# Two lanes of TensorE without zero padding, in a kernel of gated attention followed by a token mixer

## The chip, the cores and the metric

The kernel runs on one core of a Trainium2 chip. That core has TensorE (PE in the profile, with its weight loads listed apart as PEld), VectorE (DVE), ScalarE (ACT), GpSimd (POOL) and SyncE (SP, which here issues DMAs), and 16 DMA engines that move data between main memory and the core's SBUF. TensorE writes its results to PSUM, which has eight banks of 128 rows x 512 fp32 columns here. The metric is the device time of one execution in microseconds (us).

## The reference: what is computed

There are 8 batches of 3200 tokens with 256 features. The first half is an attention without softmax, gated by `u`; the second mixes tokens through two projections:

```
scores = (1/S) * z @ z.T            # z: 3200 x 64 per batch
x      = u * (relu(scores)**2 @ v)  # u, v: 3200 x 256
wq, wk = x @ w_q, x @ w_k           # 256 -> 64
mixed  = ((1/8) * wq @ wk.T) @ x
out    = relu(mixed) @ w_out        # 256 -> 256
```

The output is fp32. The kernel doesn't build `wq @ wk.T`: it sums `wk.T @ x` (64 x 256, called heads) over the tokens of a batch and multiplies `wq` with it.

## The kernel before

**Tiles.** The tokens of a batch are 25 tiles of 128. The columns of the score matrix are taken in groups of 512 (six per batch, and a last one of 128). For a group and a tile of rows, TensorE makes a 128 x 512 block of scores (`scores`, L273, matmul at L284). Two blocks share a buffer `sc` of two PSUM banks. VectorE or ScalarE moves the buffer out with relu and a scale (`first_stage`, L298 or L296, into `g`), and GpSimd or ScalarE squares it to fp16 (`second_stage`, L309 or L307, into `at`). As the score matrix is symmetric, some blocks are got by a transposing DMA from an earlier one (`tt`).

**The second product.** For each group, `second_product` (L432) sums over all 25 tiles of rows: the squared scores are the weights, `v_sb` the moving operand, 256 columns per matmul. A group of 512 fills two accumulator banks, `acc0` and `acc1`. All the recorded matmuls of this kind, and those of the extras below, stand under L346, the `emit` of an item; their tiles tell them apart. When a group closes, `gate` (L456) multiplies the accumulators with `u`: VectorE takes `acc0` (L475), ScalarE copies `acc1` (L474) and GpSimd multiplies it. The next group uses the same two banks, so its first matmul waits for both.

**Two lanes.** Most matmuls use 64 of TensorE's 128 rows: the lower half of a tile's rows is one lane (LOW), the upper half the other (HIGH), and a matmul of one lane runs beside one of the other if they write different banks. So `lanes` (L373) emits a list of items twice. In the first pass lane LOW takes the items of one bank and HIGH those of the other; in the second they change over, so that each bank gets both halves of the rows. `swap_after` (L411) puts between the passes a wait for the last matmul of either lane. The two matmuls of a score buffer are one per lane too, LOW first.

**Extras.** Besides scores and the second product a step may carry one extra, written to a buffer of the same pool as the scores (three buffers, `ps_tile`): `project` (L735) is the last product with `w_out`; `keys_and_heads` (L744) holds the two projections of a group of `x` in one bank (two items of 512 columns, 1024 in all) and in the other the heads of an earlier group (items of 256, mostly four of them) with, at times, the projections of the batch's last 128 tokens or a small remainder of the batch before (`side`). This other bank has 1024 columns or 1280, 1536 or, once, 2048. Where it is not 1024, `evened` (L361) puts items of 128 columns with zeros for the moving operand ahead of the last item of the shorter list, at most four.

**Order of the work.** The schedule is written out by the kernel itself: the instructions of each engine stand in the order in which the program emits them. A loop over 169 steps decides for each what is due. A step emits, in this order: some pairs of scores (`heading` of them, L958 to 961), the squares that are due, then the matmuls of the second product and the extra by `run` (L398), which walks a list of emitters and drops `asides`, the remaining score pairs among them, at given shares of the list's width (`shares_of`, L853). A step that begins a group and has an extra of both banks emits both passes of the extra first, then those of the group; one in the middle of a group puts the first pass of the extra inside the first pass of the group. A step of a batch's last group (128 columns, "split") gives each lane its own partial sum and bank, so that only the extra changes banks there. `on_lanes` (L952) tells the steps that work in this way.

The order of the two lanes within one pass is by column: `lanes` keeps a counter for each lane that begins at zero in each pass, and sorts by it:

```
for i in evened(banks, lane ^ across):
    todo.append((at, lane, i, rows))
    at += width(i)
```

Of the kernel before, what the change touches and what calls it, by code (L numbers as in the profile page):

```python
# [16 lines left out]
def kernel(  # L17
# [15 lines left out]
    P = 128  # L33
    NT = S // P
    ND = D // P
    W = 512
# [162 lines left out]
    zeros = consts.tile([P, P], FP16, tag="zeros", name="zeros")  # L199
# [45 lines left out]
    for b in range(B):  # L245
        for gi in range(NG):
# [23 lines left out]
    NTILE = len(tiles)  # L270
    made, turned = {}, {}

    def scores(p0):  # L273
        pair = tiles[p0 : p0 + 2]
        sc = ps_tile("sc")
        ats = [[], []]
        for h, (b, gi, tis) in enumerate(pair):
            w = widths[gi]
            half = h * dqk
            for i in range(W // w):  # L280
                ti = tis[min(i, len(tis) - 1)]
                ats[h].append((i * w, h, w, b, ti, starts[gi], half))
        for at, h, w, b, ti, gs, half in sorted(ats[0] + ats[1]):
            nc.tensor.matmul(  # L284
                out=sc[:, h, at : at + w],
                lhsT=zT[b][half : half + dqk, ds(z_at(b, h) + ti * P, P)],
                rhs=zT[b][half : half + dqk, ds(z_at(b, h) + gs, w)],
                start=True,
                stop=True,
            )  # L290
        return sc
# [48 lines left out]
    class Item:  # L340
        def __init__(self, out, lhsT, rhs, start=False, stop=False):
            self.out, self.lhsT, self.rhs = out, lhsT, rhs
            self.start, self.stop = start, stop

        def emit(self, rows, start, stop):
            return nc.tensor.matmul(  # L346
                out=self.out, lhsT=self.lhsT(rows), rhs=self.rhs(rows), start=start, stop=stop
            )
# [6 lines left out]
    def width(i):  # L355
        n = 1
        for d in i.out.shape[1:]:
            n *= d
        return n

    def evened(banks, mine):  # L361


        items = list(banks[mine])
        more = sum(map(width, banks[1 - mine])) - sum(map(width, items))
        if more > 0 and items:
            z_ = Item(
                out=items[-1].out[:, 0:P], lhsT=items[-1].lhsT, rhs=lambda r: zeros[r, :]
            )
            items[-1:-1] = [z_] * (min(W, more) // P)  # L370
        return items

    def lanes(banks, across, second, ends_):  # L373


        todo = []
        for lane, rows in enumerate((LOW, HIGH)):
            at = 0
            for i in evened(banks, lane ^ across):
                todo.append((at, lane, i, rows))  # L380
                at += width(i)

        def emit(lane, i, rows):
            ends_[lane] = i.emit(rows, i.start and not second, i.stop and second)

        return [
            (width(i) / 2, lambda lane=lane, i=i, rows=rows: emit(lane, i, rows))
            for _, lane, i, rows in sorted(todo, key=lambda x: x[:2])
        ]

    def both_lanes(banks):
        return [
            (width(i) / 2, lambda i=i, rows=rows: i.emit(rows, i.start, i.stop))
            for both in zip(*banks)
            for i, rows in zip(both, (LOW, HIGH))
        ]

    def run(emits, asides_):  # L398


        total, done = sum(n for n, _ in emits), 0
        asides_ = sorted(asides_, key=lambda x: x[0])
        for n, fn in emits:
            while asides_ and asides_[0][0] * total <= done:
                asides_.pop(0)[1]()
            fn()
            done += n
        for _, fn in asides_:
            fn()
# [426 lines left out]
    def key_due(k):  # L836
# [53 lines left out]
    def each(fns):  # L890
        for fn in fns:
            fn()
# [36 lines left out]
    across = False  # L929
# [3 lines left out]
    while groups:  # L933
# [3 lines left out]
        n = 6  # L937
# [7 lines left out]
        if mix_due(k):  # L945
# [3 lines left out]
            n = 4  # L949
# [87 lines left out]
        if on_lanes:  # L1037
            split = is_split(b, gi)
            if extra and not all(extra[0]):
                for fn in whole(extra[0]):  # L1040
                    fn()
                extra[1]()
                extra = None
            parts = [] if split else [banks]
            if extra and not begins and not split:
                n_ = max(2, min(len(banks[0]) - 2, len(banks[0]) // 2))
                parts = [[bank[:n_] for bank in banks], extra[0], [bank[n_:] for bank in banks]]
            elif extra:
                parts.insert(0, extra[0])
            emits = []  # L1050
            apart = extra and begins and not split
            if apart:
                turned_ = {}
                emits += lanes(extra[0], across, False, turned_)
                first_done = sum(n for n, _ in emits)
                emits.append((0, lambda: swap_after(turned_.values())))
                emits += lanes(extra[0], not across, True, {})
                emits.append((0, extra[1]))
                parts = [banks]
            firsts = [{} for part in parts]  # L1060
            for part, ends_ in zip(parts, firsts):
                emits += lanes(part, across, False, ends_)
            if len(parts) == 3:
                parts, firsts = [extra[0], banks], firsts[1:]
            cut = len(rows_) // 4
            if split:
                emits += both_lanes([bank[:cut] for bank in banks])
            halves_ = sum(n for n, _ in emits)
            if parts:
                across = not across  # L1070
            for part, ends_ in zip(parts, firsts):
                emits.append((0, lambda ends_=ends_: swap_after(ends_.values())))
                emits += lanes(part, across, True, {})
                if extra and not apart and part is extra[0]:
                    emits.append((0, extra[1]))
            if split:
                emits += both_lanes([bank[cut:] for bank in banks])
            at_ = shares(begins, closes, split, len(between_))
            if apart:
                all_ = sum(n for n, _ in emits)  # L1080
                at_ = [(n - 1) / all_ for n in (first_done, halves_, halves_)][: len(between_)]
            todo = [(x, lambda p0=p0: stage(p0, scores(p0))) for x, p0 in zip(at_, between_)]
            for x in acts[1:]:
                todo.append((0.5 - 1e-6, lambda x=x: each(second_stage(*x))))
            run(emits, todo)
# [158 lines left out]
```

## Time and profile before

| | |
|---|---|
| runs shown | 784.98, 785.11 and 782.51 us, median 784.98 |
| the profiled execution | 782.56 us, span of its instructions 780.7 us |
| granted TensorE clock | 0.998 of full speed |
| matmuls | 12690, busy 768.5 us |
| matmuls of zeros under L346 | 148 (104 with `wkq`, 44 with `wqk`) |
| DMA | 147.05 MB, q1 86.3% of 16 engines' span |

The span is shorter than the execution by 1.9 us that lie around it. A group of the profile names line, engine, operation, the tile written and those read, the shape (64*128 means 64 rows in use and 128 columns of weights; 64x256 is the moving operand) and the count; then the busy time, the mean time of one in ns, and the engine's idle time ahead of them. Matmuls are pipelined: one of 256 columns is recorded with 269 ns, but the next of the same lane starts 0.109 us after it. The timeline merges equal neighbours: start, length, then the operation and its count; in square brackets, the idle time before it and what ended it.

### The profile page before, as it was taken

Reading aid. Unit: us, or ns where it says so; the run is one execution under the profiler, and the core shown is the slowest. Engines: PE = TensorE matmul, PEld = TensorE weight load, DVE = VectorE, ACT = ScalarE, POOL = GpSimd, SP = SyncE. Lnnn points to the kernel's source line nnn. Section 1 sums busy time; section 2 is a strip of 40 time slices with the busy share of each in tenths; the row PEclk is TensorE's granted clock in tenths of the full one; section 3 lists DMA queues with packets and bytes.
Section 4 is the critical chain, followed back from the end, with each engine's and each line's share of the span. In section 5 each row is a group of like instructions: output and inputs, shape, how many; then the busy total and the mean of one; then the engine's idle time right before and its main releaser. Section 6 shows DMA issues by size and latency. Waiting matters only on the chain. (4 is left out here: it accounts for less than half of the span.)

```text
span 780.7 us, 28613 instructions
## 1 busy us (share of the span) xinstructions
PE 768.5 (98%) x12690; PEld 627.3 (80%) x12690; DVE 473.5 (61%) x457; ACT 556.9 (71%) x655; POOL 554.9 (71%) x363
## 2 busy tenths in 40 slices
PE   8999999999999999999999999999999999999996
PEld 6788877888788887888878887788878888888884
DVE  7654676556756577555766557655575646665444
ACT  7666787767768786685867667758696877685465
POOL 7897797758765678765879668876777546875450
PEclk9999999999999999999999999999999999999999
DMA  8999699896999479994899959999499994987626
GB/s 172 173 221 231 132 211 188 172 185 127 237 180 230 123 166 221 229 256 112 186 203 239 219 143 217 203 221 245 99 218 183 255 205 94 211 193 151 160 68 254
DMA packets 276267, 147.05 MB, mean 188 GB/s; under 512 B 252080, under 2 KB 255664, under 8 KB 276144
## 3 DMA queue, kind: packets, MB, share of 16 engines
q1 hardware_dynamic: 275424, 143.33, 86.3%
q0 software_dynamic: 576, 1.64, 1.2%
q8 instruction: 99, 1.62, 0.9%
q14 instruction: 24, 0.20, 0.1%
q10 hardware_dynamic: 144, 0.26, 0.1%
HBM read 59.38 MB, written 26.21 MB: 110 GB/s over the span
## 5 line engine op out<-in xcount | busy, mean ns | idle before, releaser
L298 DVE TENSOR_SCALAR g<-sc 128x1024 f32<-128x1024 f32 x338 | 410.7, 1223 | 241.7 <-PE sc L284 227.7
L309 POOL TENSOR_TENSOR at<-g 128x1024 f16<-128x1024 f32 x238 | 448.0, 1894 | 122.9 <-DVE g L298 100.1
L346 PE MATMUL acc<-v_sb,at 64*128 64x256 f16 (+1 forms) x7387 | 474.5, 269 | 1.8 <-DVE x_sb L475 0.7
L346 PEld LDWEIGHTS <-at 64*128 64x128 f16 (+1 forms) x7387 | 364.9, 94 | 87.4 <-PE acc L346 25.0
L307 ACT ACTIVATE at<-g 128x1024 f16<-128x1024 f32 x230 | 239.2, 1055 | 29.4 <-DVE g L298 17.6
L346 PE MATMUL acc<-v_sb,tt 64*128 64x256 f16 (+1 forms) x2540 | 174.8, 269 | 0.0
L284 PE MATMUL sc<-zT 64*128 64x512 f16 (+1 forms) x1104 | 168.6, 344 | 1.6 <-ACT g L296 0.8
L296 ACT ACTIVATE g<-sc 128x1024 f32<-128x1024 f32 x130 | 133.0, 1023 | 41.4 <-PE sc L284 39.3
L346 PEld LDWEIGHTS <-tt 64*128 64x128 f16 (+1 forms) x2540 | 127.2, 94 | 15.0
L477 POOL TENSOR_TENSOR x_sb<-gt,u_sb 128x512 f16<-128x512 f32 x48 | 61.2, 1275 | 72.7 <-ACT gt L474 65.3
L611 ACT ACTIVATE rt<-mx 128x1024 f16<-128x1024 f32 x47 | 47.8, 1023 | 34.4 <-PE mx L590 32.3
L284 PEld LDWEIGHTS <-zT 64*128 64x128 f16 x1104 | 55.5, 94 | 11.2 <-issue 3.9
L474 ACT COPY gt<-acc 128x512 f32<-128x512 f32 x48 | 28.1, 585 | 48.6 <-PE acc L346 48.5
L346 PE MATMUL fo<-wo,rt 64*128 64x256 f16 (+1 forms) x688 | 58.2, 270 | 0.1
L346 PE MATMUL qk<-x_sb,kx 64*128 64x256 f16 x368 | 55.2, 269 | 0.0
L512 ACT CAST qk<-qk 128x512 f16<-128x512 f32 x47 | 27.5, 586 | 37.3 <-PE qk L346 37.2
L475 DVE TENSOR_TENSOR x_sb<-acc,u_sb 128x512 f16<-128x512 f32 x48 | 33.1, 690 | 26.7 <-PE acc L346 25.3
L346 PEld LDWEIGHTS <-rt 64*128 64x128 f16 (+1 forms) x688 | 35.9, 94 | 15.2 <-PE fo L346 5.1
L672 ACT ACTIVATE fo<-fo 128x1024 f32<-128x1024 f32 x39 | 39.9, 1024 | 4.3 <-PE fo L346 4.3
L346 PEld LDWEIGHTS <-kx 64*128 64x128 f16 (+1 forms) x386 | 35.5, 94 | 7.6 <-PE qk L346 0.9
L346 PE MATMUL qk<-xT_sb,wkq 64*128 64x512 f16 (+1 forms) x90 | 31.8, 377 | 0.0
L346 PE MATMUL qk<-xT_sb,wqk 64*128 64x512 f16 (+1 forms) x94 | 30.1, 377 | 0.0
(81 smaller groups left out, 268.9 us busy)
## 6 DMA issues: line engine op xcount, KB each, us to landing
u_sb<-in_u_dram SPq DMA_DIRECT2D x48, 512.0 KB, 5.1
out_dram<-fo SPq DMA_DIRECT2D x45, 512.0 KB, 3.4
piece<-in_v_dram SPq DMA_DIRECT2D x42, 512.0 KB, 4.6
piece<-in_z_dram SPq DMA_DIRECT2D x7, 512.0 KB, 5.9
tt<-at SPq DMA_TRANSPOSE x162, 4.8
piece<-in_z_dram SPq DMA_DIRECT2D x7, 288.0 KB, 5.5
out_dram<-fo SPq DMA_DIRECT2D x5, 256.0 KB, 2.7
u_sb<-in_u_dram SPq DMA_DIRECT2D x8, 128.0 KB, 3.3
```

The source lines that it names most:

```text
L284: nc.tensor.matmul(out=sc[:, h, at : at + w], lhsT=zT[b][half : half + dqk, ds(z_at(b, h) + ti * P, P)], rhs=zT[b][half : half + dqk, ds(z ...
L296: nc.scalar.activation(out=g[:], in_=sc[:], func=RELU, scale=GSCALE)
L298: nc.vector.tensor_scalar(out=g[:], in0=sc[:], scalar1=0.0, scalar2=GSCALE, op0=AOP.max, op1=AOP.mult)
L307: nc.scalar.square(out=out, in_=g[:])
L309: nc.gpsimd.tensor_mul(out=out, in0=g[:], in1=g[:])
L346: return nc.tensor.matmul(out=self.out, lhsT=self.lhsT(rows), rhs=self.rhs(rows), start=start, stop=stop)
L474: nc.scalar.copy(out=upper[:], in_=accs[1][:])
L475: nc.vector.tensor_mul(out=x[:, 0:n], in0=accs[0][:, 0:n], in1=ug[:, 0:n])
L477: nc.gpsimd.tensor_mul(out=x[:, n : 2 * n], in0=upper[:], in1=ug[:, n : 2 * n])
L512: nc.scalar.copy(out=qks[b, gi][:, 0:gw], in_=out)
L611: nc.scalar.activation(out=out, in_=ps[:], func=RELU)
L672: nc.scalar.mul(out=flat_out[:, sl], in_=part, mul=FINAL_SCALE)
```

## The change

Three things are changed. `evened` goes, and with it the zeros. The emitters of a step are no longer lists that are joined: a new class, `Streams`, keeps one counter of columns for each lane over the whole step and sorts all matmuls by the column at which their lane can begin them; `first_pass` and `second_pass` add the two passes of a part, and a second pass doesn't begin before the column at which both lanes have ended the first one. A step that begins a group with an extra of unequal banks now adds the first pass of the extra, the first pass of the group, the second pass of the extra and the second pass of the group; with equal banks the order is as it was.

The score pair of an aside begins with the lane that has been given fewer columns so far (`lead`). For a step that begins a group with keys and heads, the share of the first aside is 0.0 instead of 0.5, and one more pair of scores goes ahead of the step if a `side` is waiting.

```diff
-    def scores(p0):
+    def scores(p0, lead=0):
...
-        for at, h, w, b, ti, gs, half in sorted(ats[0] + ats[1]):
+        for at, h, w, b, ti, gs, half in sorted(ats[0] + ats[1], key=lambda x: (x[0], x[1] ^ lead)):
...
-    def evened(banks, mine):
-        items = list(banks[mine])
-        more = sum(map(width, banks[1 - mine])) - sum(map(width, items))
-        if more > 0 and items:
-            z_ = Item(
-                out=items[-1].out[:, 0:P], lhsT=items[-1].lhsT, rhs=lambda r: zeros[r, :]
-            )
-            items[-1:-1] = [z_] * (min(W, more) // P)
-        return items
-    def lanes(banks, across, second, ends_):
...
-    def both_lanes(banks):
...
+    class Streams:
+        def __init__(self):
+            self.at, self.todo = [0, 0], []
+        def add(self, lane, n, fn):
+            self.todo.append((self.at[lane], len(self.todo), n, lane, fn))
+            self.at[lane] += n
+        def aside(self, at, fn):
+            self.todo.append((at, len(self.todo), 0, 0, fn))
+        def ordered(self):
+            return [x[2:] for x in sorted(self.todo, key=lambda x: x[:2])]
+    def first_pass(streams, banks, across):
+        ends_ = {}
+        def emit(lane, i, rows):
+            ends_[lane] = i.emit(rows, i.start, False)
         for lane, rows in enumerate((LOW, HIGH)):
...
+            for i in banks[lane ^ across]:
+                streams.add(lane, width(i), lambda lane=lane, i=i, rows=rows: emit(lane, i, rows))
+        return banks, across, max(streams.at), ends_
+    def second_pass(streams, first):
+        banks, across, done, ends_ = first
+        streams.at = [max(at, done) for at in streams.at]
+        streams.aside(min(streams.at), lambda: swap_after(ends_.values()))
+        for lane, rows in enumerate((LOW, HIGH)):
+            for i in banks[1 - (lane ^ across)]:
+                streams.add(lane, width(i), lambda i=i, rows=rows: i.emit(rows, False, i.stop))
+    def uneven(extra):
+        a, b = (sum(map(width, bank)) for bank in extra[0])
+        return a != b
...
+    def run(streams, asides_):
+        todo = streams.ordered()
+        total, done = sum(x[0] for x in todo), [0, 0]
         asides_ = sorted(asides_, key=lambda x: x[0])
...
+        for n, lane, fn in todo:
+            while asides_ and asides_[0][0] * total <= sum(done):
+                asides_.pop(0)[1](int(done[1] < done[0]))
             fn()
...
+            done[lane] += n
...
-        "bk": (0.5, 0.5, 0.5),
+        "bk": (0.0, 0.5, 0.5),
...
+            if begins and keying and side: heading += 1
...
+            if split:
+                cut = len(rows_) // 4
+                if extra:
+                    first = first_pass(streams, extra[0], across)
+                    across = not across
+                each_lane(streams, [bank[:cut] for bank in banks])
+                if extra:
+                    extra_second(first)
+                each_lane(streams, [bank[cut:] for bank in banks])
+            elif extra and begins and uneven(extra):
+                first_extra = first_pass(streams, extra[0], across)
+                first = first_pass(streams, banks, across)
+                extra_second(first_extra)
+                second_pass(streams, first)
+                across = not across
...
             elif extra:
...
                 n_ = max(2, min(len(banks[0]) - 2, len(banks[0]) // 2))
...
+                first = first_pass(streams, [bank[:n_] for bank in banks], across)
+                first_extra = first_pass(streams, extra[0], across)
+                first = (banks, across) + first_pass(streams, [bank[n_:] for bank in banks], across)[2:]
+                extra_second(first_extra)
+                second_pass(streams, first)
                 across = not across
```

More of the change, by code (lines that the diff above doesn't have):

```diff
@@ L402, in run, with each_lane @@
+    def uneven(extra):
+        a, b = (sum(map(width, bank)) for bank in extra[0])
+        return a != b
+    def each_lane(streams, banks):
+        for lane, rows in enumerate((LOW, HIGH)):
+            for i in banks[lane]:
+                streams.add(lane, width(i), lambda i=i, rows=rows: i.emit(rows, i.start, i.stop))
+    def run(streams, asides_):
+        todo = streams.ordered()
+        total, done = sum(x[0] for x in todo), [0, 0]
         asides_ = sorted(asides_, key=lambda x: x[0])
-        for n, fn in emits:
-            while asides_ and asides_[0][0] * total <= done:
-                asides_.pop(0)[1]()
+        for n, lane, fn in todo:
+            while asides_ and asides_[0][0] * total <= sum(done):
+                asides_.pop(0)[1](int(done[1] < done[0]))
@@ L406, in run @@
             fn()
-            done += n
+            done[lane] += n
         for _, fn in asides_:
-            fn()
+            fn(0)
     def swap_after(ends_):
@@ L1043 @@
                 extra = None
-            parts = [] if split else [banks]
-            if extra and not begins and not split:
-                n_ = max(2, min(len(banks[0]) - 2, len(banks[0]) // 2))
[L1047 to L1069, printed above, removed]
-                across = not across
[L1071 to L1082, printed above, removed]
+            streams = Streams()
+            at_ = shares(begins, closes, split, len(between_))
@@ new lines, in extra_second @@
+            def extra_second(first):
+                second_pass(streams, first)
+                streams.aside(max(streams.at) - 1, extra[1])
+            if split:
[13 more added lines that the diff above has]
+                across = not across
+            elif extra and begins:
+                first = first_pass(streams, extra[0], across)
+                marks = [max(streams.at)]
+                extra_second(first)
+                first = first_pass(streams, banks, across)
+                marks.append(max(streams.at))
+                second_pass(streams, first)
+                across = not across
+                marks = [2 * x for x in marks]
+                total = sum(x[2] for x in streams.todo)
+                at_ = [(x - 1) / total for x in marks + marks[1:]][: len(between_)]
+            elif extra:
+                n_ = max(2, min(len(banks[0]) - 2, len(banks[0]) // 2))
+                first = first_pass(streams, [bank[:n_] for bank in banks], across)
+                first_extra = first_pass(streams, extra[0], across)
+                first = (banks, across) + first_pass(streams, [bank[n_:] for bank in banks], across)[2:]
+                extra_second(first_extra)
+                second_pass(streams, first)
+                across = not across
+            else:
+                second_pass(streams, first_pass(streams, banks, across))
+                across = not across
@@ L1083 @@
+            todo = [(x, lambda lead, p0=p0: stage(p0, scores(p0, lead))) for x, p0 in zip(at_, between_)]
             for x in acts[1:]:
-                todo.append((0.5 - 1e-6, lambda x=x: each(second_stage(*x))))
-            run(emits, todo)
+                todo.append((0.5 - 1e-6, lambda lead, x=x: each(second_stage(*x))))
+            run(streams, todo)
         else:
```

18 lines of the change are left out of this document (removed).

## The prediction

> **What bounds the kernel now.** I read the page's busy line first, then the chain of waits of TensorE, then the groups kept apart by shape, and last the timeline around the steps that the change touches.
>
> The page's busy line and two groups (columns: count, busy us, mean ns of one, idle before):
>
> ```profile
> PE 768.5 (98%) x12690; PEld 627.3 (80%) x12690; DVE 473.5 (61%) x457; ACT 556.9 (71%) x655; POOL 554.9 (71%) x363
> ...
> L346 PE MATMUL qk<-zeros,wkq 64*128 64x128 f16 x104 | 12.2, 216 | 0.0
> L346 PE MATMUL qk<-zeros,wqk 64*128 64x128 f16 x44 | 5.3, 216 | 0.0
> ```
>
> PE is busy 98% and the other engines 61 to 71%. PE's waits add up to 4.7 us (1.0, 0.8, 0.7, 0.5, 0.5, 0.4, 0.2 in the waits view). So a column that PE need not stream is time, unless a wait grows in its place. There are 104 + 44 = 148 products of zeros. The 216 ns are latency, not price; the price is the distance between starts. The timeline of PE shows it (start, length, operation, count):
>
> ```profile
> 366.28 0.38 PE L346 MATMUL qk<-xT_sb,wkq 64*128 64x512 f16 x1
> 366.28 0.38 PE L346 MATMUL qk<-x_sb,kx 64*128 64x256 f16 x2
> 366.49 0.22 PE L346 MATMUL qk<-zeros,wkq 64*128 64x128 f16 x1
> 366.50 0.27 PE L346 MATMUL qk<-x_sb,kx 64*128 64x256 f16 x1
> 366.55 0.27 PE L346 MATMUL qk<-zeros,wkq 64*128 64x128 f16 x2
> 366.61 0.27 PE L346 MATMUL qk<-x_sb,kx 64*128 64x256 f16 x1
> 366.66 0.22 PE L346 MATMUL qk<-zeros,wkq 64*128 64x128 f16 x1
> 366.72 0.38 PE L346 MATMUL qk<-xT_sb,wkq 64*128 64x512 f16 x1
> 366.72 0.38 PE L346 MATMUL qk<-wo,rs 64*128 64x256 f16 x2
> 366.93 1.04 PE L346 MATMUL acc<-v_sb,tt 64*128 64x256 f16 x16
> ```
>
> One lane streams 512 columns, four zeros and 512 columns while the other streams six products of 256; both reach the accumulation at 366.93. From the starts: 0.056 us per 128 columns, 0.109 per 256 (366.50 to 366.61), 0.216 per 512. Starts of the two lanes that interleave, as here, keep the same 0.109 that lanes in step have.
>
> **The change part by part.** (1) The zeros. Every extra with banks of unequal width is run twice, the lanes swapping banks, so each lane got half of the zeros: 148 / 2 x 0.056 = 4.1 us per lane is the most they can be worth. Where they stand, from the built order of both kernels: 22 steps in the middle or at the end of a group (15 with 256 columns of difference, that is four zeros, and 7 with 512, eight zeros), five steps that begin a group (at 138, 229, 258, 661 and 678 us), and two steps of a split last group (at 179 and 272.5 us).
>
> Middle steps: 15 x 4 + 7 x 8 = 116 zeros, 58 x 0.056 = 3.25 us. Nothing waits inside them and each lane goes on into its accumulation, so I take all of it. In the new order at least seven matmuls (0.38 us) stand between the last product that a change of banks waits for and that change, against two (one score pair, 0.22) in most steps now, so no drain is laid open.
>
> Steps that begin a group. Here the first pass of the accumulation now comes right after one pass of the extra, and the score pair that stood between the passes moves to the front:
>
> ```profile
> 228.67 0.38 PE L284 MATMUL sc<-zT 64*128 64x512 f16 x2
> 228.86 0.69 DVE L475 TENSOR_TENSOR x_sb<-acc,u_sb 128x512 f16<-128x512 f32 x1 [0.88 <-PE acc L346]
> 228.88 0.38 PE L346 MATMUL qk<-xT_sb,wkq 64*128 64x512 f16 x1
> 228.95 0.59 ACT L474 COPY gt<-acc 128x512 f32<-128x512 f32 x1 [0.80 <-PE acc L346]
> ```
>
> The accumulators are free when DVE's multiply ends: 228.86 + 0.69 = 229.55, and PE sees it 0.05 to 0.06 later, 229.61 (at the split step DVE ends at 178.81 + 0.69 = 179.50, and the accumulation that waits for it starts at 179.55). Now PE comes to them at 230.23, covered. After: scores 228.67 and 228.89, extra from 229.10, the lane with 1024 columns is at the accumulators at 229.53: a wait of 0.08. The zeros there are worth 0.11 per step (two per lane). At 138 and 258 us the same rows give the same 0.08; at 678 DVE ends at 678.61 (677.92 + 0.69) and the lane is there at 678.55: 0.11. Four steps: 0.45 - 3 x 0.08 - 0.11 = 0.10 us. Only one lane waits, so the bounds are 0.1 and 0.45. The extra's evacuation comes later (at 229 about 0.4 us): the casts of ACT queue behind it, and DVE's sum of heads now stands behind a third eviction; ACT's next idle time there is 1.83 us, so it is hidden. At 661 it waits about 1.3 us and the idle time behind is 2.24. If that cover were gone the next eviction, and so PE, would be late by the difference.
>
> The step at 661 is the one that loses:
>
> ```profile
> 659.32 2.35 DVE L298 TENSOR_SCALAR g<-sc 128x1024 f32<-128x1024 f32 x2 [0.26 <-PE sc L284]
> ...
> 660.50 0.39 PE L284 MATMUL sc<-zT 64*128 64x512 f16 x2
> 660.71 0.27 PE L346 MATMUL qk<-x_sb,kx 64*128 64x256 f16 x1
> ...
> 661.73 0.39 PE L284 MATMUL sc<-zT 64*128 64x512 f16 x2
> ```
>
> There are three PSUM buffers for scores and extras. DVE empties two, the second at 659.32 + 2.35 = 661.67. Now the extra takes the first and runs a pass before the second score needs the second, at 661.73. In the new order the score takes the first and the extra waits from 660.50 + 0.43 = 660.93 to 661.73: 0.80 us. By walking both orders to the second pass of the accumulation, from the same start 660.50: now 664.58 (the row of the trace); after 661.73 + 8 x 0.109 (heads) + 14 x 0.109 + 0.216 + 0.43 = 664.78. So 0.20 slower, though eight zeros and 0.21 us of idle lane go. Bounds: 0.45 gained with no wait, 0.8 lost.
>
> Split steps. At 179 the accumulation waits for DVE either way, until 179.55: nothing. At 272.5 one more score pair is put ahead; the zeros give 0.11, and a wait goes too: the last product of the extra starts at 272.97 + 0.056, ends its columns at 273.09, and the accumulation starts at 273.30. The 0.216 of scores fill that: 0.31 together.
>
> (2) The share of steps that begin a group with an extra: in two early ones (51 and 65 us) a score pair moves ahead of the accumulation, which now waits for DVE. At 51: extra from 51.40 in 2 x 0.216, accumulation at 52.03, 0.2 later; some 0.1 of it is the change from whole to half rows (score at 51.09 + 0.216, extra only at 51.40). I take 0.1 each, 0.2 together; bounds 0 and 0.4.
>
> (3) The lane that leads in a score pair. Six pairs outside the steps above change their order; in the timeline their rows are 0.47 or 0.48 long instead of 0.38. One of them now:
>
> ```profile
> 573.36 0.49 PE L346 MATMUL acc<-v_sb,at 64*128 64x256 f16 x5
> 573.58 0.48 PE L284 MATMUL sc<-zT 64*128 64x512 f16 x2
> 573.80 1.03 PE L346 MATMUL acc<-v_sb,at 64*128 64x256 f16 x15
> ```
>
> The fifth accumulation keeps its lane from 573.58 to 573.69. The score of that lane is issued first, yet a score starts at 573.58: it is the other lane's, issued second, and 0.216 later that lane goes on. So each lane takes its next product by itself, no time is lost, and the new order gains 0.
>
> The Trainium skill says otherwise (TensorE: Matmul & The Clock Gate, Part 3: Packing small matmuls): matmuls start in strict program order, only weight loads are pulled ahead. By that rule 573.58 to 573.69 would be lost now in both lanes, and the six pairs would give 4 x 0.106 + 2 x 0.09 = 0.6 us more. This trace disagrees with it in its starts.
>
> Sum: 3.25 + 0.10 - 0.20 + 0.31 + 0.20 = 3.66 us. What no row shows is whole passes with the lanes 256 or 512 columns apart. The nearest row is the interleaved stretch above, which costs nothing. The far bound is the first pair behind a score, which can start 0.226 instead of 0.216 after it: 10 ns on some 12 pairs in each of 22 steps, 2.6 us. A gain from it is excluded, since the columns remain. I take nothing, the row nearest to it.
>
> The profiled execution took 782.56 us (span 780.7 and 1.9 around it), so it would be 778.9. The runs shown are 784.98, 785.11 and 782.51, median 784.98; with the profiled one they lie in two pairs 2.5 us apart. Against the middle of the four, 783.8, the sum gives 780.1, which I forecast.
>
> **The rivals.** (a) Half of it is lost to waits that the sum does not see: at 56 beginnings of groups the accumulators come free by DVE and ACT, DMA engines are 86% busy, and a PE that is 0.1 us earlier waits 0.1 us longer. For it: 0.08 and 0.11 above arise in this way. Against it: PE's waits are 4.7 us in all, and these chains start from PE itself. 783.8 - 1.8 = 782.0. (b) The change doesn't save what it says, since out of step the lanes cost the 10 ns per pair: 783.8 - 3.66 + 2.6 = 782.7. (c) Slower: a change of banks is laid open. Price: at 664.12 a score takes one lane, 0.216, and that lane's next accumulation starts at 664.58, so 0.24. In the 29 steps there are 58 changes; 15 laid open undo the gain, 58 give 783.8 - 3.66 + 13.9 = 794. Against it stand the seven matmuls between. (d) Matmuls in strict order, if the second start of a pair, 0.09 to 0.10 late in those six rows, were lost time: 0.6 is gained on top, 779.5. Against it: 573.80 follows 573.58 by a score's 0.216.
>
> **How the numbers follow.** Forecast 0.60, (a) 0.17, (b) 0.07, (c) 0.06, (d) 0.10. A measurement of this kernel can tell about 0.5%, 3.9 us, from no change. The likeliest case alone lies between 777.7 (lower pair of runs, gate waits of one lane not counted) and 781.5 (upper pair). The range goes to (a) and (b) from the upper pair, and to (d) without the loss at 661 below: 776.9 to 783.5. Faster by over 0.5% is 781.1 or less against the median: most of the forecast and of (d), 0.59. Within 0.5%: the rest of them, (a) and (b), 0.34. Slower: (c) and a little of (b), 0.07.
>
> **What would show it.** No products of zeros and 12542 matmuls; PE busy some 4 us less; at 366 the accumulation 0.22 us after the second product of 512; a wait of about 0.8 ahead of the extra at 661 and of 0.1 at three or four beginnings. Wrong would be: waits of PE well above 4.7 us at the beginnings, gaps of 0.24 at bank changes, or pairs of 256 columns more than 0.109 apart where the lanes have drifted.

## The result and the profile after

The changed kernel takes 779.06 us, the median of 8 runs (778.41 to 782.66); the kernel before takes 783.40 us, the median of 8 runs on the same chip (782.51 to 785.11). The ratio is 0.9953, with a 95% interval of 0.9933 to 0.9973: 0.47% faster, and so at the edge of what a measurement of this kernel can tell. The profiled execution of the changed kernel took 779.59 us, with a span of 777.7, against 782.56 and 780.7.

The page's busy line of the changed kernel (engine, busy us, share of the span, number of instructions):

```profile
PE 764.8 (98%) x12542; PEld 628.2 (81%) x12542; DVE 472.8 (61%) x457; ACT 557.4 (72%) x655; POOL 555.4 (71%) x363
```

The 148 products of zeros are gone (12690 - 148 = 12542), PE's busy time is 3.7 us less, and its share is still 98%. The waits of PE (what waited for what: us in all, times, longest) tell where something took their place:

```profile
PE sc L895 <- DVE zeros L932: 1.0, 1, 1.0
PE acc L346 <- DVE x_sb L484: 0.7, 4, 0.2
PE qk L346 <- DVE g L298: 0.6, 1, 0.6
PE ztp L129 <- POOL zd L120: 0.6, 1, 0.6
PE sc L284 <- DVE g L298: 0.5, 1, 0.5
PE qq L346 <- DVE fo L1218: 0.5, 1, 0.5
PE sc L284 <- ACT g L296: 0.3, 1, 0.3
PE mx L599 <- ACT rt L620: 0.2, 1, 0.2
PE sc L284 <- ACT rt L620: 0.2, 1, 0.2
```

They add up to 4.6 us, against 4.1 before. There the lines for `zeros`, `x_sb`, DVE's `g`, `fo` and `mx` have the same totals as here, and the other two are

```profile
PE sc L284 <- ACT g L296: 0.8, 2, 0.6
PE ztp L129 <- POOL zd L120: 0.4, 1, 0.4
```

Two lines are new: `qk` waits 0.6 for DVE's `g`, which is the extra at 661, and a score pair waits 0.2 for ACT's `rt`, behind the step at 678. The waits for the accumulators (`x_sb`) are 0.7 in both.

The timeline of PE in the changed kernel, at the middle step that stood at 366 before (start, length, operation, count):

```profile
365.06 0.38 PE L346 MATMUL qk<-xT_sb,wkq 64*128 64x512 f16 x1
365.07 0.38 PE L346 MATMUL qk<-x_sb,kx 64*128 64x256 f16 x2
365.28 0.38 PE L346 MATMUL qk<-xT_sb,wkq 64*128 64x512 f16 x1
365.29 0.38 PE L346 MATMUL qk<-x_sb,kx 64*128 64x256 f16 x2
365.50 0.27 PE L346 MATMUL acc<-v_sb,tt 64*128 64x256 f16 x1
365.50 0.27 PE L346 MATMUL qk<-wo,rs 64*128 64x256 f16 x1
365.61 0.27 PE L346 MATMUL acc<-v_sb,tt 64*128 64x256 f16 x1
365.61 0.27 PE L346 MATMUL qk<-wo,rs 64*128 64x256 f16 x1
365.71 0.82 PE L346 MATMUL acc<-v_sb,tt 64*128 64x256 f16 x12
```

The second product of 512 starts 0.22 after the first, and 0.22 after it its lane is in the accumulation, two matmuls ahead of the other. The starts stay 0.109 apart.

**Where the time went, step by step.** In both traces 56 groups close, each with a DVE instruction that takes the accumulators; the last, which writes another tile, is left out here, so there are 55 closings. The time between two closings is repeatable to 0.01 us wherever the work between them is the same (behind the first 80 us), so differences of 0.1 us can be read off although whole runs scatter by some us. The table gives, for the stretches between closings, what the changed kernel takes against the kernel before:

| stretch (time of before) | measured, us | predicted, us |
|---|---|---|
| start to the first closing (24 us), same order on PE | +0.60 | 0 |
| closing at 38 to closing at 51, same order on PE | -0.10 | 0 |
| the two early steps, 51 and 65 | -0.07, -0.08 | -0.20 together |
| 14 middle steps with 256 columns of difference | -0.11 or -0.12 each | -0.112 each |
| 7 middle steps with 512 columns | -0.22 or -0.23 each | -0.224 each |
| begin steps at 138, 229, 258 | -0.10, -0.10, -0.09 | -0.03 each |
| begin step at 678 and the middle step behind it (256 columns), one stretch | -0.10 | -0.11 |
| begin step at 661 | +0.19 | +0.20 |
| split steps at 179, 272.5 | 0.00, -0.32 | 0, -0.31 |
| first to last closing, sum | -4.01 | -3.66 |
| last closing to PE's end | 0.00 (18.77 both) | 0 |
| PE's end to the last transfer's end | +0.44 (6.87 against 6.42) | 0 |

The span is so 0.60 - 4.01 + 0.44 = 3.0 us less. The first and the last line of these three are not the change's: in the profiled executions of the experiments below the first closing lay anywhere between 23.6 and 25.7 us with the same instructions on PE, in one odd order at 30.6. The gain between the closings is the 4.0. Of it, 0.10 is not the change's either: the stretch from 38 to 51 has the same order in both kernels, and PE waits there 0.21 for ACT's eviction in the kernel before. So the change is worth about 3.9.

The stretch from 678 hides more than its -0.10 shows. From its closing, the extra of the middle step begins 0.06 (one lane) to 0.10 (the other) earlier than before, and `mx` behind that step 0.17 to 0.21 earlier; the begin step thus gained up to 0.1 and the middle step its 0.11. Then a score pair, at 689.13 in the changed kernel, waits 0.19 for ACT's `rt`, and 0.10 of the gain is lost again.

### The profile page after: what moved, and what is told of

It is laid out like the page before. It is cut to its first block, busy times and chain, and to the rows that moved or that the text cites. A ratio compares the mean times of both kernels' runs of the same rounds, so it can differ in the third digit from the quotient of the medians.

```text
span 777.7 us, 28318 instructions
## 1 busy us (share of the span) xinstructions
PE 764.8 (98%) x12542; PEld 628.2 (81%) x12542; DVE 472.8 (61%) x457; ACT 557.4 (72%) x655; POOL 555.4 (71%) x363
## 5 line engine op out<-in xcount | busy, mean ns | idle before, releaser
L346 PEld LDWEIGHTS <-at 64*128 64x128 f16 (+1 forms) x7387 | 368.7, 94 | 83.9 <-PE acc L346 24.5
L346 PE MATMUL acc<-v_sb,tt 64*128 64x256 f16 (+1 forms) x2540 | 178.6, 269 | 0.0
L284 PE MATMUL sc<-zT 64*128 64x512 f16 (+1 forms) x1104 | 170.4, 345 | 1.2 <-DVE g L298 0.5
L296 ACT ACTIVATE g<-sc 128x1024 f32<-128x1024 f32 x130 | 133.1, 1024 | 42.9 <-PE sc L284 40.8
L346 PEld LDWEIGHTS <-tt 64*128 64x128 f16 (+1 forms) x2540 | 129.0, 94 | 14.8
L620 ACT ACTIVATE rt<-mx 128x1024 f16<-128x1024 f32 x47 | 47.9, 1024 | 31.9 <-PE mx L599 30.0
L681 ACT ACTIVATE fo<-fo 128x1024 f32<-128x1024 f32 x39 | 40.0, 1024 | 4.3 <-PE fo L346 4.3
L346 PE MATMUL qk<-xT_sb,wqk 64*128 64x512 f16 (+1 forms) x94 | 27.9, 377 | 0.0
L346 PE MATMUL qk<-xT_sb,wkq 64*128 64x512 f16 (+1 forms) x90 | 26.7, 376 | 0.0
```

The lines of the kernel that those rows point to most:

```text
L284: nc.tensor.matmul(out=sc[:, h, at : at + w], lhsT=zT[b][half : half + dqk, ds(z_at(b, h) + ti * P, P)], rhs=zT[b][half : half + dqk, ds(z ...
L296: nc.scalar.activation(out=g[:], in_=sc[:], func=RELU, scale=GSCALE)
L346: return nc.tensor.matmul(out=self.out, lhsT=self.lhsT(rows), rhs=self.rhs(rows), start=start, stop=stop)
L620: nc.scalar.activation(out=out, in_=ps[:], func=RELU)
L681: nc.scalar.mul(out=flat_out[:, sl], in_=part, mul=FINAL_SCALE)
```

## The experiments

They are compared by the same closings, in one profiled execution each. Three of them were also timed in several runs.

**1. Only the zeros out.** The kernel before, with no products of zeros and everything else as it was; the shorter lane idles until the longer one is done with its pass.

```diff
-            items[-1:-1] = [z_] * (min(W, more) // P)
+            items[-1:-1] = []
```

> The kernel before with nothing changed but that no zeros are added; the old order stays. Theory (each lane goes through its own matmuls by itself, and a lane drifts wherever no change of banks holds it): all of the 3.25 us of the 22 middle steps, 0.11 or 0.23 each, and nothing at the seven other steps, where the shorter lane only waits at the change of banks or for VectorE: 3.2 to 3.3 us less than before from the first closing of a group to the last. Rival (the new order is what lets the lanes drift): the steps keep most of their length, less than 1 us in all. Rival (matmuls start in the order in which they are issued): the 15 steps with 256 columns gain, the 7 with 512 lose about half of theirs, 2.4 us.

Measured: 780.75 us (779.33 to 781.84, 6 runs) against 783.25, ratio 0.9966 (0.9953 to 0.9979). From the first to the last closing it takes 3.41 us less than the kernel before (3.30 without the stretch from 38 to 51, where 3.2 to 3.3 was expected) and 0.60 more than the changed one. In 19 of the 22 stretches with a middle step it equals the changed kernel to 0.01 us, and in a twentieth, at 375, it is 0.03 more and in the next stretch 0.03 less: there the old sort, lane by lane from the start of each pass, already lets the lanes drift into the accumulation. The new order is worth something only where it puts other work between the passes: at the begin steps 138, 229 and 258 (0.07 to 0.08 each), at the early steps (0.06 and 0.08) and at the split step at 272.5 (0.24, and 0.08 in the stretch behind it). The stretch from 678, with a begin step and a middle one, is 0.09 longer without it. At 661 the new order is worse by 0.19.

Why taking the zeros out alone gives nearly nothing at a begin step is in the timeline of this experiment at the step that was at 229:

```profile
228.97 0.38 PE L284 MATMUL sc<-zT 64*128 64x512 f16 x1
228.97 0.27 PE L346 MATMUL qk<-xTl,wkq 64*128 64x128 f16 x2
229.09 0.38 PE L284 MATMUL sc<-zT 64*128 64x512 f16 x1
229.31 0.28 PE L346 MATMUL qk<-x_sb,kx 64*128 64x256 f16 x1
```

The lane that has no `xTl` begins its score at 228.97 and is done at 228.97 + 0.216 = 229.19; it must then wait for the other lane before the second pass, until 229.31. Without zeros it idles for the 0.11 that the zeros took.

**2. The zeros back in the new order.** The changed kernel, with `evened` as it was, called on the lists of `first_pass` and `second_pass`.

```diff
-            for i in banks[lane ^ across]:
+            for i in evened(banks, lane ^ across):
...
-            for i in banks[1 - (lane ^ across)]:
+            for i in evened(banks, 1 - (lane ^ across)):
```

> The changed kernel with the products of zeros put back where they were, in the new order. Theory (the gain is the zeros' columns): the 22 middle steps take 0.11 or 0.22 us more again, 3.25 in all, the steps at 138, 229 and 258 us 0.11 more each less what the wait for the accumulators hides (0 to 0.1 each), so 3.3 to 3.7 us slower than the changed kernel. Rival (the gain comes from the order, the share and the lead): under 1 us slower.

Measured: 782.40 us in one run, span 780.5. It is 3.62 us slower than the changed kernel from the first to the last closing: 0.11 or 0.22 in the stretch of each middle step but the one at 678 (0.05), 0.04 at the begin steps 138, 229 and 258, 0.11 at 272.5 and 0.22 at 661. Against the kernel before, which has the same zeros, it shows what the order is worth by itself: 0.07, 0.07 and 0.05 less at the begin steps 138, 229 and 258, 0.07 and 0.08 less at the early steps, 0.21 less at 272.5, 0.41 more at 661, and nothing in the middle steps. The price of a zero, 0.056 us per lane, is thus the same in both orders, which rules out that lanes out of step pay 10 ns per pair: that rival would have made the removal worth a fraction of it. At 661 the eight zeros cost their full price in the new order, so the 0.19 lost there is the place of the passes, not the zeros.

**3. The lead taken away.** The changed kernel, with LOW first in every score pair.

```diff
-                asides_.pop(0)[1](int(done[1] < done[0]))
+                asides_.pop(0)[1](0)
```

> The changed kernel, but a score pair always begins with the lower lane, as before. Theory (a lane takes its next matmul by itself): within 0.1 us of the changed kernel from the first closing of a group to the last. Rival (strict order of issue): each of the six pairs, and those of the drifting steps, lose about 0.1 us: 0.6 to 2 us slower.

Measured: 778.21 us in one run, span 776.3; 0.11 us more than the changed kernel from the first to the last closing, with no step over 0.01. The lead is worth 0.1 at most. The pair that the prediction showed at 573.58 stands in the changed kernel at 571.00:

```profile
570.77 0.49 PE L346 MATMUL acc<-v_sb,at 64*128 64x256 f16 x5
571.00 0.48 PE L284 MATMUL sc<-zT 64*128 64x512 f16 x2
571.21 1.03 PE L346 MATMUL acc<-v_sb,at 64*128 64x256 f16 x15
```

Its row is still 0.48 long. The two starts lie apart because the lanes are apart, whichever is issued first.

**4. Issue order without column order.** The changed kernel, with the sorted matmuls of both lanes taken in fours (then sixes, eights, sixteens) and within each such chunk all of LOW before all of HIGH: mostly two (three, four, eight) of a lane in a row.

```diff
-            return [x[2:] for x in sorted(self.todo, key=lambda x: x[:2])]
+            out, held = [], []
+            for x in [x[2:] for x in sorted(self.todo, key=lambda x: x[:2])]:
+                if x[0]:
+                    held.append(x)
+                if not x[0] or len(held) == 4:
+                    out += sorted(held, key=lambda y: y[1])
+                    held = []
+                if not x[0]:
+                    out.append(x)
+            return out + sorted(held, key=lambda y: y[1])
```

Two at a time: 

> The changed kernel, but the matmuls of the two lanes in a step are issued two of the lower lane, then two of the upper, instead of in turn. Theory: no change, within 0.3 us. Rival (strict order of issue): the second of the lower lane waits for the first, and the upper lane stands behind it, so four matmuls take three turns of 0.109 us instead of two: on 5436 of 256 columns per lane about 290 us more.

Eight at a time: 

> The same with eight of the lower lane, then eight of the upper. Theory (each lane by itself, as far as the queue of issued instructions reaches): if it reaches past sixteen matmuls with their weight loads, no change; if it is shorter than eight, time between that and strict order, about 15 turns instead of 8, 500 us more. No theory says which of these; under strict order it is 500 us.

Three at a time: 

> Three matmuls of one lane issued, then three of the other. Two at a time cost 2.25 us from the first to the last closing, eight at a time 91. If a lane's matmul may start while up to some number k of the other lane's stand unstarted ahead of it, and each one beyond k costs the wait for its start (0.109 us), then the cost rises from a bend: with a bend at 2 this run loses about a third to a half of what a strict order would cost, some 20 to 40 us; with a bend at 4 or more it stays below 5 us.

Four at a time: 

> The same with four at a time. With a bend at 2: 40 to 70 us more than the changed kernel; with a bend at 4 or more: below 8 us; if the cost simply grows with the number at a time between the two runs known (2.25 at two, 91 at eight): about 30 us.

| in a row | time of the one run, us | first to last closing, against the changed kernel |
|---|---|---|
| 1 (changed kernel) | 779.59 | 0 |
| 2 | 781.12 | +2.25 |
| 3 | 780.16 | +2.01 |
| 4 | 786.85 | +8.1 |
| 8 | 876.37 | +91.3 |

The prices that I had set for a strict order of starts, 290 us with two and 500 with eight, were wrong: they left out that the next products of LOW can start together with the last of HIGH. Worked out again, n in a row take 2(n - 1) turns of 0.109 us instead of n, apart from what is lost where the lanes meet at a change of banks. For 5436 products per lane that is nothing with two in a row, some 200 us with three, 300 with four and 440 with eight. So the run with two says little about strict order by its time. The run with three does: it cost 2.01. Its starts show it directly, at the begin step of 229:

```profile
228.29 0.38 PE L346 MATMUL qk<-xT_sb,wkq 64*128 64x512 f16 x1
228.30 0.38 PE L346 MATMUL qk<-x_sb,kx 64*128 64x256 f16 x2
228.50 0.38 PE L346 MATMUL qk<-xT_sb,wkq 64*128 64x512 f16 x1
```

LOW's two `xT_sb` are issued ahead of HIGH's `x_sb`, yet the first `x_sb` starts at 228.30, before the second `xT_sb` at 228.50. So the lanes do go by themselves, but only over a few matmuls of issue: four in a row cost 8.1, and eight 91. How many matmuls they reach exactly these runs, one each, don't tell, since one lane may stay behind the other from chunk to chunk. My numbers missed at two (I had expected at most 0.3) and, by a little, at four (at most 8).

Part of what two and four cost is not the reach but a wait. It stands in the timeline of the run with four in a row, at the begin step of 229:

```profile
230.74 0.59 PE L346 MATMUL qk<-xT_sb,wkq 64*128 64x512 f16 x2
231.25 0.27 PE L346 MATMUL acc<-v_sb,at 64*128 64x256 f16 x1
231.25 0.39 PE L346 MATMUL qk<-x_sb,kx 64*128 64x256 f16 x2
```

LOW's accumulation waits for DVE's multiply, which began at 230.50 (230.50 + 0.69 + 0.06 = 231.25). HIGH's `qk<-x_sb` waits for nothing and could have begun at 230.74 with LOW's extra, yet it starts at 231.25 too, as it is issued behind the waiting one. A matmul that waits for another engine holds back both lanes; one that only waits for its lane does not. This step lost 0.49 with four, 0.24 with two in a row.

**5. The bank change laid open.** The changed kernel, with the extra's second pass right behind its first one in the middle steps, instead of a part of the accumulation between them.

```diff
                 first_extra = first_pass(streams, extra[0], across)
+                extra_second(first_extra)
                 first = (banks, across) + first_pass(streams, [bank[n_:] for bank in banks], across)[2:]
-                extra_second(first_extra)
```

> The changed kernel, but in the middle steps with an extra the second pass of the extra follows straight on its first, so that nothing stands ahead of that change of banks. It prices the rival that a change of banks is laid open. Theory: 0.24 us for each such step, less what a lane that is ahead has waited already, and where banks are unequal the shorter lane idles 0.11 or 0.22 besides: 0.24 to 0.35 per middle step. Rival (a change of banks costs nothing even with no cover): no more than 0.05 per step.

Measured: 803.32 us in one run, 22.8 us more from the first to the last closing: in most stretches with one middle step and an extra, 0.47 or 0.48 with even banks, 0.58 with 256 columns of difference, 0.69 with 512. I had counted one change of banks per step; the timeline shows two:

```profile
373.40 0.38 PE L346 MATMUL qk<-xT_sb,wkq 64*128 64x512 f16 x1
373.40 0.38 PE L346 MATMUL qk<-x_sb,kx 64*128 64x256 f16 x2
373.62 0.38 PE L346 MATMUL qk<-wo,rs 64*128 64x256 f16 x2
374.06 0.28 PE L346 MATMUL qk<-x_sb,kx 64*128 64x256 f16 x1
374.06 0.39 PE L346 MATMUL qk<-xT_sb,wkq 64*128 64x512 f16 x1
...
375.16 0.82 PE L346 MATMUL acc<-v_sb,tt 64*128 64x256 f16 x10
376.04 0.83 PE L346 MATMUL acc<-v_sb,at 64*128 64x256 f16 x12
```

The longer lane streams its last two items from 373.62 to 373.84, and the second pass begins at 374.06: 0.22. The group's own change, with nothing moved between its passes any more, is laid open as well: the last product of that row starts at 375.16 + 0.82 - 0.27 = 375.71 and streams until 375.82, and the second pass begins at 376.04, again 0.22. The shorter lane idles besides for its 0.11 or 0.22. Price: 0.24 per change, as the prediction took it from the row at 664. What keeps the changed kernel from paying it is the part of the accumulation that stands between.

**6. The two places where the new order gave nothing.** The changed kernel, with one more score pair ahead of the split steps without a `side` (at 92 and 179), and at 661 the order of passes that even banks have.

```diff
-            if begins and keying and side: heading += 1
+            if begins and keying and (side or is_split(*groups[0])): heading += 1
...
-        return a != b
+        return 0 < abs(a - b) < 1024
```

> The changed kernel with two repairs: one more pair of scores ahead of every split step that begins with keys and heads (there are three, at 92, 179 and 272 us, of which the last has it already), and the old order of passes, without zeros, at the step at 661 us whose banks differ by 1024 columns. Theory: 0.2 us less at 92 and 0.2 to 0.3 at 179, where the accumulators are waited for, and 0.1 to 0.3 less at 661, where the extra no longer waits for VectorE's second eviction: 0.5 to 0.8 us less than the changed kernel. Rival (these waits are followed by others that absorb them): under 0.2 us.

Measured: 780.38 us (778.74 to 782.47, 5 runs) against 784.63, ratio 0.9947 (0.9924 to 0.9970). From the first to the last closing it takes 0.24 us less than the changed kernel: 0.22 less at 92, 0.21 less at 179, as expected, but 0.10 more at 661, where I had expected 0.1 to 0.3 less. The timeline there:

```profile
657.08 0.71 PE L346 MATMUL qk<-x_sb,kx 64*128 64x256 f16 x5
657.84 0.39 PE L346 MATMUL qk<-xT_sb,wqk 64*128 64x512 f16 x1
658.07 0.38 PE L284 MATMUL sc<-zT 64*128 64x512 f16 x2
```

The five products start from 657.08 to 657.52 and stream until 657.63; the second pass begins 0.21 later, at 657.84, with nothing between, and only then comes the score pair. It is a bank change laid open again. The pair's place is marked as twice the columns of the longer lane, which is right for even banks only.

**7. The same with the places counted over both lanes.**

```diff
-                marks = [max(streams.at)]
+                marks = [sum(x[2] for x in streams.todo)]
...
-                marks.append(max(streams.at))
+                marks.append(sum(x[2] for x in streams.todo))
...
-                marks = [2 * x for x in marks]
+                marks = list(marks)
```

> As the run that gave the split steps a score pair and the step at 661 its old order of passes, but with the two places for score pairs in that step counted by the columns of both lanes together, so that a pair stands after the first and after the second pass of the extra, at each of its two changes of banks. From the first to the last closing of a group: theory (the 0.10 us lost at 661 in that run came from a change of banks laid open, because the pair fell into the second pass): the step at 661 gains about 0.2 us against the changed kernel, the sum with the split steps is about 0.6 us less than the changed kernel, 4.6 less than the kernel before. Rival (the order with equal banks is itself no better with uneven ones): the step stays at +0.1, and the sum at about -0.24.

Measured: 778.33 us (778.27 to 783.55, 5 runs) against 784.08, ratio 0.9932 (0.9910 to 0.9954). At 661 it takes 0.21 us less than the changed kernel, at 92 and 179 0.22 and 0.21: 0.64 together, as expected. The score pair now stands between the passes:

```profile
661.94 0.71 PE L346 MATMUL qk<-x_sb,kx 64*128 64x256 f16 x5
662.63 0.39 PE L284 MATMUL sc<-zT 64*128 64x512 f16 x2
662.85 0.27 PE L346 MATMUL qk<-x_sb,kx 64*128 64x256 f16 x1
```

Its profiled execution was the slowest of the five, 783.55 us. Over the whole of it the sum can't be read, for two stretches with the same instructions were longer than in the changed kernel: 0.95 us between the closings at 38 and 51, and 4.04 between those at 65 and 78. ACT's waits in it show what was late. A square on ACT, at 36.92, stood 5.1 us for a transposing DMA (at most 2.8 in the changed kernel), and PE waited 1.1 us for the eviction behind it. Another, at 65.25, stood 4.6 us for nothing that the profile shows, and PE waited 2.3 us for the eviction behind that one. With those two stretches left out, the kernel is 0.52 us ahead of the changed one from the first to the last closing. By its steps it is the best of the three, by 0.64 us over the changed kernel; by whole runs that can't be told, as the runs of either scatter by 4 to 5 us.

## Why the prediction was right

The forecast was 780.1 us; the median is 779.06. The sum was 3.66 us of gain, the trace shows 4.0 between the first and the last closing, 3.9 of it by the change, and the medians differ by 4.34. The step from 3.9 to 4.34 is not explained by these traces; it is within the scatter of the runs. Of the 1.0 us by which the forecast was too long, 0.4 is its starting point (783.8, where the kernel before then took 783.40).

**Middle steps, 3.25 predicted.** Right, in total and in each: 0.11 and 0.22, 3.3 together, though what the one at 687 gained was mostly lost again, as a wait behind it took 0.10 back. The zeros' price was read from the distance of starts, not from the 216 ns of the row, which would have made 148 / 2 x 0.216 = 16 us. That the lanes out of step cost nothing was argued from the interleaved rows at 366; experiment 2 shows it.

**Begin steps, 0.10 predicted for four.** This is the term that was mis-sized: three gave 0.29, and the fourth, at 678, up to 0.1 that was lost again behind it. The wait was there as worked out. The timeline of the changed kernel:

```profile
228.54 0.59 PE L284 MATMUL sc<-zT 64*128 64x512 f16 x4
228.74 0.69 DVE L484 TENSOR_TENSOR x_sb<-acc,u_sb 128x512 f16<-128x512 f32 x1 [0.88 <-PE acc L346]
228.98 0.38 PE L346 MATMUL qk<-xT_sb,wkq 64*128 64x512 f16 x1
229.42 0.22 PE L346 MATMUL qk<-xTl,wkq 64*128 64x128 f16 x1
229.49 0.27 PE L346 MATMUL acc<-v_sb,at 64*128 64x256 f16 x1
229.49 0.23 PE L346 MATMUL qk<-xTl,wkq 64*128 64x128 f16 x1
```

DVE ends at 228.74 + 0.69 = 229.43; the lane that has streamed 1024 columns was there at 228.98 + 2 x 0.216 = 229.41 and starts at 229.49, 0.08 late. The other lane stood too: its second `xTl` starts with the accumulation that was waiting, 0.02 late. Still the step gained 0.10, not 0.03. Experiment 2 divides it: the zeros account for 0.04, about what the sum has for them (0.11 less the wait of 0.08), and the new order for 0.05 to 0.07, which the prediction put at nothing. Part of that stands in the rows of the kernel before:

```profile
229.43 0.38 PE L284 MATMUL sc<-zT 64*128 64x512 f16 x2
229.67 0.28 PE L346 MATMUL qk<-x_sb,kx 64*128 64x256 f16 x1
```

The second pass of the extra begins 0.24 after the score pair, whose columns take 0.216, so one pair did not quite cover the change of banks; at the next change the distance is 0.23 (232.19 to 232.42). In the new order the accumulation stands ahead of the change, and the extra's second pass follows its score pair by 0.21 to 0.22. Where the rest of the 0.07 comes from is not shown.

**The step at 661, a loss of 0.20 predicted.** Right: 0.19. The changed kernel's timeline:

```profile
656.16 2.35 DVE L298 TENSOR_SCALAR g<-sc 128x1024 f32<-128x1024 f32 x2 [0.26 <-PE sc L284]
657.34 0.61 PE L284 MATMUL sc<-zT 64*128 64x512 f16 x4
658.57 0.27 PE L346 MATMUL qk<-x_sb,kx 64*128 64x256 f16 x1 [0.62 <-DVE g L298]
```

DVE empties the second buffer at 656.16 + 2.35 = 658.51; the extra could have begun at 657.34 + 0.43 = 657.77 and begins at 658.57, the 0.80 us that were worked out. Experiments 1 and 7 have the old order of passes at this step and no such loss.

**The split steps, 0 and 0.31 predicted.** Right: 0.00 and 0.32. Experiment 6 shows that the gain at 272.5 is the score pair ahead of it: the same pair gave 0.21 to 0.22 at the two steps that hadn't got one.

**The early steps, 0.20 predicted, and the lead, 0.** The early steps gave 0.15, the lead at most 0.1.

**The rivals.** (a), half of it lost to waits at the beginnings of groups, fell: PE waits 0.7 us for the accumulators in both traces. The prediction's 4.7 us of waits was a wrong sum of its own seven figures, which make 4.1; they rose to 4.6, with the 0.6 at 661 as the largest new one, and not by 1.8. (b), 10 ns per pair, fell by experiment 2. (c), bank changes laid open, had the right price (0.24 by experiment 5, 0.21 of it seen in experiment 6), but the middle steps of the changed kernel gave the full price of their zeros, so no change is open there. (d), strict order, fell by experiments 3 and 4: the Trainium skill (TensorE: Matmul & The Clock Gate, Part 3: Packing small matmuls) has matmuls start in program order, and for matmuls of different lanes the starts measured here don't: three in a row of each lane cost 2.01 us and not some 200, and `x_sb` at 228.30 started before the `xT_sb` issued ahead of it.

The two profiled executions differ by only 2.97 us, since 0.60 at the start and 0.44 at the last transfer went against the change; the medians differ by 4.34.

## What to carry to other kernels

When two lanes share an engine, padding that keeps them in step costs its columns and buys nothing here; what has to be kept is work between the passes, so that a change of banks finds the last products drained (0.24 us each otherwise). Look for steps in which the new order brings a matmul earlier to a buffer that is not yet free: one such step, of 29 that were changed, gave back 0.19 us, where the whole change is worth 3.9. Ask too what an earlier TensorE will meet further on: at 689 a wait for ScalarE took back 0.10. And when a gain is smaller than the scatter of whole runs, compare the traces between marks that recur, where the same work repeats to 0.01 us.

## What the runs showed of the hardware

- The two lanes start their matmuls without regard to each other's order of issue, but over a short way: two or three in a row of one lane cost 2.0 to 2.3 us in all, four 8.1, eight 91.
- A matmul that waits for another engine holds both lanes: HIGH's product, which waited for nothing, started with LOW's accumulation at 231.25 rather than at 230.74.
- With nothing between, a change of banks costs 0.24 us (0.47 or 0.48 for two in a step). One score pair, 0.216 us of columns, covers it but for some 0.02: the next pass began 0.24 after the pair's start (229.43 to 229.67).
- The same instructions took 23.6 to 25.7 us to the first closing, and a transposing DMA or a stall of 4.6 us on ACT with no cause in the profile moved single stretches of the first 80 us by 1 to 4 us; from there on stretches repeat to 0.01.
